# Attention and two gated MLPs in one kernel: the order of the first pairs and its loads, a conversion of float64 weights, and a priority at the end

## The chip, the cores and the metric

The kernel runs on one core of a Trainium2 chip. The metric is the time of one execution on the device in microseconds (us): 707.32 us, the median of three runs before the change (706.92 to 711.9).

## The reference

Three stages follow one another, for 4 batches of 576 positions with width 512.

- Attention with 8 heads of width 64. Heads 0 to 3 see the last 32 positions (local), heads 4 to 7 the earlier positions of the same residue modulo 32 (strided).
- A gated block: `h = gelu(x @ w_in)`, cut into halves u and v; v is normalised and mixed along the positions, `v_s = w_sg @ v_n + b_sg`; the result is `x + (u * v_s) @ w_out`.
- A plain block: `x + relu(norm(x) @ w_ch1) @ w_ch2`, with an inner width of 2048.

The inputs are float32. The weights w_in, w_out, w_ch1 and w_ch2 reach the kernel as float64 words.

## The kernel before, in words

**Matrix products.** Each large operand is split into a high and a low fp32r part (`split`, lines 175 to 181), and a product is three matmuls (`mm3`, lines 203 to 205): low by high, high by low, high by high. Nearly all of TensorE's (PE's) time goes into these.

**Attention** works on pairs of heads, p = 0 and 1 local, p = 2 and 3 strided, per batch. `attn_load` (l) loads queries and keys of a pair into a tile `qk`, 592 KB for a local pair and 601 KB for a strided one; `attn_load_v` (m) loads its values, 432 or 384 KB. `attn_s` (s) makes the scores in two PSUM banks: for batch 0 the mask is written into the bank first, as a matmul of the identity `ident_r` by `mask_lr` or `mask_sr`, with start=True, and the 36 or 44 small products of queries and keys are added. VectorE (DVE) reduces each bank to row maxima (L378), and subtracts them (L380) for p = 0, 2 and 3. `attn_e` (e) takes the exponential on ScalarE (ACT; L394, or L399 one block at a time for p = 1), the row sums (L395), and scales the rows (L402 to L409). `attn2` (x) transposes on PE (L438), copies on ACT (L446), multiplies with the values (L457, L474) and splits the result into `xhl`. Of `qk`, `v` and `pt` there are two buffers each.

**Start of the kernel.** The string START gives the program order of the first steps of batch 0: the letters above with the number of the pair, `w` (load, convert and split one of four 512 KB tiles of w_in for the v half), `v` (12 matmuls of 512 columns for four row blocks with that tile, into four PSUM banks of the pool ps_d), and `c` (constants). START_D names the pairs whose scores use ps_d's four banks instead of ps_s's two. The loads of a step are issued on SyncE's (SP's) queue. With the first pair go four pieces of its queries and keys (the first five blocks of queries, the same of keys, then the rest of both), and ident (64 KB) and mask_l (96 KB) after the first two; mask_s (27 KB) goes in `load_consts`.

**The order on the engines.** A planner puts the instructions of each engine, and the DMA issues of SP, in order when the kernel is built. It goes by the program order as priority and by its own model of when operands and buffers are there; `tc.high_priority(offset=100)` moves the instructions inside it ahead by 100 places in that priority. On the chip each engine runs its list in that order, so an instruction that waits holds up all behind it on its engine. PE's weight loads may run ahead of its matmuls.

**Weights.** `from_f64` (lines 183 to 198) turns a float64 word, read as two 32-bit words, into a float32: ACT takes the absolute value of the high word times 2^-112 (L190), DVE shifts it left by 3 (L193), puts back the sign bit of the high word (L194), and puts in the top three bits of the low word (L196). It is called 8 times for w_in, 8 for w_out (half as wide), 23 times for w_ch1 and w_ch2, and 18 times at half width in `pre_w`, which converts some of these early and stores them in DRAM.

**The rest.** After the start, four loops per batch run: v (five row blocks), u (8 groups), g (8 groups, needs all of wsg) and y (8 groups); the attention of the next batch is put between them at places given by PLACE0 and PLACE. From about 330 us on only the plain block is left: `ch1` and `ch2_mm` in turn for six column chunks of 384 positions; at the end of a chunk `ch2_out` (line 755) multiplies each of four PSUM sums by the reciprocal norm (L757), adds the residual (L759), and stores the last ones (L761).

Of the kernel before, what the change touches and what calls it, by code (L numbers as in the profile page):

```python
# [24 lines left out]
P = 128  # L25
# [49 lines left out]
    6, "x", 3))  # L75
START = "l0 m0 c0 l1 m1 s0 s1 l2 w0 e0 e1 m2 w1 x0 l3 m3 s2 e2 s3 x1 v0 x2 e3 w2 v1 c1 x3 w3 v2 v3"
CUT = 1
START_D = (1, 2)
F64_SCALE = 2.0 ** -112
NCHUNK = NT // CH  # L80
TPC = CH // P
# [65 lines left out]
def mixer_kernel(ctx: ExitStack, tc: tile.TileContext, io, out):  # L147
# [36 lines left out]
    def from_f64(raw, w, src, k, queue=nc.sync, after=None):  # L184
        if src is not None:
            queue.dma_start(out=raw.rearrange("p (k f) -> p k f", k=k), in_=src)
        r3 = raw.rearrange("p (n w) -> p n w", w=2)
        low, high = r3[:, :, 0], r3[:, :, 1]
        wf = w.bitcast(F32)
        first = nc.scalar.activation(wf, high.bitcast(F32), AF.Abs, scale=F64_SCALE)  # L190
        if after is not None:
            tc.add_manual_dep(first.ins, after.ins.name, ORDER, reason="spare time")
        nc.vector.tensor_scalar(out=w, in0=w, scalar1=3, scalar2=None, op0=ALU.logical_shift_left)  # L193
        nc.vector.scalar_tensor_tensor(out=w, in0=high, scalar=0x80000000, in1=w,  # L194
                                       op0=ALU.bitwise_and, op1=ALU.bitwise_or)
        nc.vector.scalar_tensor_tensor(out=w, in0=low, scalar=29, in1=w,  # L196
                                       op0=ALU.logical_shift_right, op1=ALU.bitwise_or)
        return wf.rearrange("p (k f) -> p k f", k=k)
# [35 lines left out]
    def load_consts():  # L234
        nc.sync.dma_start(out=mask_s, in_=io["mask_s"])
        nc.vector.tensor_copy(mask_sr, mask_s)
        nc.vector.memset(neghalf, -0.5)
        nc.vector.memset(eps, 1e-6)
        nc.vector.memset(one.bitcast(F32), 1.0)
        for t in pts:  # L240
            nc.vector.memset(t.rearrange("p (n w) -> p n w", w=SLOT)[:, :, GW:], 0.0)
        nc.vector.memset(vn[64:128, 1, 4, :].bitcast(F32), 1.0)

    def load_w_v(kk):
        raw, w = slot()
        f = from_f64(raw, w, io["w_in"][kk * P:(kk + 1) * P, 2 * WP:4 * WP].unsqueeze(1), 1)
        split(winh[:, kk, WP:], winl[:, kk, WP:], f[:, 0, :])
# [46 lines left out]
    def attn_load(b, p):  # L294
        local = p < NP // 2
        qk = at.tile([P, max(KO + STRIDE + S, KS + NSG * GW)], F32, tag="qk", name="qk")
        kv[b, p] = qk
        src = io["qk_l" if local else "qk_s"][b, p % (NP // 2)]
        if (b, p) == (0, 0):
            cuts = (0, 5 * QB, KO, KO + STRIDE + 5 * QB, src.shape[1])  # L300
            for i in (0, 2, 1, 3):
                cs = slice(cuts[i], cuts[i + 1])
                nc.sync.dma_start(out=qk[:, cs], in_=src[:, cs])
                if i == 2:
                    nc.sync.dma_start(out=ident, in_=io["ident"])
                    nc.sync.dma_start(out=mask_l, in_=io["mask_l"])
            nc.scalar.activation(ident_r, ident, AF.Copy)
            nc.vector.tensor_copy(mask_lr, mask_l)
        else:
            nc.sync.dma_start(out=qk[:, :src.shape[1]], in_=src)  # L310
        if b:
            attn_load_v(b, p)
# [12 lines left out]
    def attn_s(b, p):  # L325
# [23 lines left out]
        mkr = mask_lr[:, 1, :] if local else mask_sr  # L349
        if on_pe:  # L350
            for sl, m, ps3, lo in todo:
                if lo:
                    nc.tensor.matmul(ps3[:, 0, :], lhsT=ident_r, rhs=mask_lr[:, 0, :], start=True, stop=False,
                                     skip_group_check=True)
                nc.tensor.matmul(ps3[:, lo:, :], lhsT=ident_r,
                                 rhs=mkr.unsqueeze(1).to_broadcast([P, m - lo, w]), start=not lo, stop=False,
                                 skip_group_check=True)
        for i in range(n):
            for h in range(2):
# [4 lines left out]
                nc.tensor.matmul(todo[i % 2][2][r0:r0 + 64, i // 2, :], lhsT=qk[hs_, q0:q0 + QB],  # L364
                                 rhs=qk[hs_, k0:k0 + w], start=not on_pe, stop=True,
                                 skip_group_check=True)
        chunks = []
        for sl, m, ps3, lo in todo:
# [386 lines left out]
    def ch2_out(c, d, f1, op_):  # L755
        r = op_.tile([P, CH], F32, tag="o", name="o")
        nc.vector.tensor_tensor(out=r, in0=accs[c, d][:, :CH], in1=rbs[c], op=ALU.mult)  # L757
        y = ys[c][:, d, :]
# [4 lines left out]
    def v_part(kk):  # L763
        for t in range(4):
            v_mm(0, t, kk)

    first = {"l": lambda p: attn_load(0, p), "m": lambda p: attn_load_v(0, p), "s": lambda p: attn_s(0, p), "e": lambda p: attn_e(0, p),
             "x": lambda p: attn2(0, p), "w": load_w_v, "v": v_part,
             "c": lambda i: load_consts() if i == 0 else nc.sync.dma_start(out=g_v, in_=io["g_v"])}
# [112 lines left out]
```

## Time and profile before

| | |
|---|---|
| median of the runs | 707.32 us |
| the profiled execution, its own time | 709.89 us |
| its span on the chip | 708.1 us |
| PE busy | 691.0 us, 98% |
| PE weight loads busy | 664.5 us, 94% |
| DVE busy | 418.7 us, 59% |
| ACT busy | 284.9 us, 40% |
| granted PE clock, mean | 0.994 |
| DMA | 61.30 MB, mean 87 GB/s |

Busy time is counted from an instruction's start to its end; PE's matmuls overlap, so a busy PE may still wait in short stretches. The share of an engine is a mean over stages that differ: DVE and ACT are busy in most of the first 350 us and little later. The span leaves out some time around the execution, 1.8 us here. The slices of the page show PE at half of the first slice of 17.7 us and at nine tenths or more from the second to the last but one.

### The profile page before, as it was taken

What the parts mean: (1) busy time and instruction counts of PE and PEld (TensorE: products, weight loads), DVE (VectorE), ACT (ScalarE), POOL (GpSimd) and SP (SyncE); (2) the same over time, 40 slices, a digit from 0 to 9 for tenths busy, and PEclk for the clock granted to TensorE, in tenths of its full rate; (3) what the DMA queues carried; (4) which work ended last, traced back from release to release, by engine and by line L of the source; (5) the groups of instructions that cost most, each with busy time, mean ns of one, the idle gap of its engine ahead of it and who ended that gap; (6) DMA issues with size and microseconds to landing.
All of it is one profiled execution on the core that took longest, in us unless ns stands there. A gap on an engine that the chain in (4) does not pass through costs nothing.

```text
span 708.1 us, 12770 instructions
## 1 busy us (share of the span) xinstructions
PE 691.0 (98%) x5206; PEld 664.5 (94%) x5206; DVE 418.7 (59%) x892; ACT 284.9 (40%) x746; POOL 25.6 (4%) x26
## 2 busy tenths in 40 slices
PE   5999999999999999999999999999999999999997
PEld 3779979989898999999999999999999999999997
DVE  4889788696877895999873257262336134413113
ACT  2877976392568463465441132131122113211110
POOL 0002011000200020001000000000000000000000
PEclk9899999999999999999999999999999999999999
DMA  8764223457343425244420020200110010001001
GB/s 252 256 192 145 81 81 125 143 164 222 120 130 106 140 88 200 76 155 134 149 90 1 0 89 23 68 1 0 48 43 1 1 45 1 1 1 45 0 1 45
DMA packets 30346, 61.30 MB, mean 87 GB/s; under 512 B 3088, under 2 KB 14352, under 8 KB 30288
## 3 DMA queue, kind: packets, MB, share of 16 engines
q1 hardware_dynamic: 30288, 60.49, 26.8%
q8 instruction: 41, 0.67, 0.4%
q14 instruction: 17, 0.14, 0.1%
HBM read 48.68 MB, written 11.80 MB: 85 GB/s over the span
## 4 chain that ended last, share of the span: by engine, by line
PE 83%; issue 4%; ACT 4%; DVE 4%; DMA 2%; POOL 1%; SPq 1%; POOLq 0%; ACTq 0%
PE ps_o L205 9%; PE ps_o L203 9%; PE ps_o L204 9%; PE ps_h L205 9%; PE ps_h L203 9%; PE ps_h L204 9%; PE ps_v L203 2%; PE ps_y L203 2%; PE ps_v L205 2%; PE ps_y L204 2%; PE ps_y L205 2%; PE ps_v L204 2%; ACT pt L399 2%; PE ps_t L438 2%; PE ps_u L203 2%
## 5 line engine op out<-in xcount | busy, mean ns | idle before, releaser
L744 DVE SCALAR_TENSOR_TENSOR h<-ps_h,h 128x384 fp32r<-128x384 f32 x96 | 52.8, 549 | 182.4 <-ACT h L743 182.2
L743 ACT ACTIVATE h<-ps_h 128x384 fp32r<-128x384 f32 x96 | 46.8, 488 | 229.9 <-PE ps_h L205 229.7
L203 PE MATMUL ps_o<-h,w 128*128 128x384 f32 x384 | 128.4, 334 | 0.0
L203 PE MATMUL ps_h<-xn,w 128*128 128x384 f32 x384 | 128.4, 334 | 0.0
L204 PE MATMUL ps_h<-xn,w 128*128 128x384 f32 x384 | 128.3, 334 | 0.0
L205 PE MATMUL ps_o<-h,w 128*128 128x384 f32 x384 | 128.3, 334 | 0.0
L205 PE MATMUL ps_h<-xn,w 128*128 128x384 f32 x384 | 128.3, 334 | 0.0
L204 PE MATMUL ps_o<-h,w 128*128 128x384 f32 x384 | 128.3, 334 | 0.0
L203 PEld LDWEIGHTS ps_o<-h,w 128*128 128x128 f32 x384 | 72.1, 188 | 0.2 <-DVE o L757 0.2
L203 PEld LDWEIGHTS ps_h<-xn,w 128*128 128x128 f32 x384 | 72.1, 188 | 0.0
L205 PEld LDWEIGHTS ps_h<-xn,w 128*128 128x128 f32 x384 | 72.1, 188 | 0.0
L204 PEld LDWEIGHTS ps_h<-xn,w 128*128 128x128 f32 x384 | 72.1, 188 | 0.0
L204 PEld LDWEIGHTS ps_o<-h,w 128*128 128x128 f32 x384 | 72.1, 188 | 0.0
L205 PEld LDWEIGHTS ps_o<-h,w 128*128 128x128 f32 x384 | 72.1, 188 | 0.0
L203 PE MATMUL ps_g<-wsg,vn 128*128 128x288 f32 x128 | 39.2, 307 | 0.3 <-ACT wsg L177 0.3
L205 PE MATMUL ps_g<-wsg,vn 128*128 128x288 f32 x128 | 38.3, 300 | 0.0
L203 PE MATMUL ps_u<-xhl,winl 128*128 128x288 f32 x128 | 38.1, 298 | 0.1
L203 PE MATMUL ps_y<-gt,wout 128*128 128x288 f32 x128 | 37.8, 298 | 0.0
L204 PE MATMUL ps_g<-wsg,vn 128*128 128x288 f32 x128 | 37.8, 296 | 0.0
L204 PE MATMUL ps_y<-gt,wout 128*128 128x288 f32 x128 | 37.7, 295 | 0.0
L205 PE MATMUL ps_u<-xhl,winh 128*128 128x288 f32 x128 | 37.7, 295 | 0.0
L205 PE MATMUL ps_y<-gt,wout 128*128 128x288 f32 x128 | 37.7, 295 | 0.0
(170 smaller groups left out, 1281.0 us busy)
## 6 DMA issues: line engine op xcount, KB each, us to landing
raw<-in_w_ch SPq DMA_DIRECT2D x23, 512.0 KB, 3.7
qk<-in_qk_s SPq DMA_DIRECT2D x8, 601.0 KB, 4.8
raw_p<-in_w_ch SPq DMA_DIRECT2D x18, 256.0 KB, 3.2
y_scratch<-y SPq DMA_DIRECT2D x16, 288.0 KB, 3.3
yT<-y_scratch SPq DMA_DIRECT2D x6, 768.0 KB, 4.7
out<-yT SPq DMA_DIRECT2D x24, 192.0 KB, 1.9
qk<-in_qk_l SPq DMA_DIRECT2D x7, 592.0 KB, 5.1
st<-in_w_in SPq DMA_DIRECT2D x8, 512.0 KB, 5.2
```

Of the source, the lines that this page charges most:

```text
L203: nc.tensor.matmul(ps, lhsT=ll, rhs=rh, start=first, stop=False)
L204: nc.tensor.matmul(ps, lhsT=lh, rhs=rl, start=False, stop=False)
L205: last_mm[0] = nc.tensor.matmul(ps, lhsT=lh, rhs=rh, start=False, stop=last)
L399: exps.append(nc.scalar.activation(p3[:, i, :], src, AF.Exp, scale=SCALE, bias=mx[:, i:i + 1], accum_out=sm[:, i:i + 1]))
L438: nc.tensor.transpose(ps[:rows, (t - t0) * c:(t - t0 + 1) * c], src, ident)
L743: nc.scalar.activation(h[:, 0, :], o, AF.Relu)
L744: nc.vector.scalar_tensor_tensor(out=h[:, 1, :], in0=o, scalar=0.0, in1=h[:, 0, :], op0=ALU.max, op1=ALU.subtract)
```

## The change

1. START has a new order, and a new step `r`, which issues the load of a w_in tile by itself; `w` then only converts. Pairs 0, 1 and 2 are loaded one after the other ahead of the first values and weights.
2. `qk` has three buffers. ident, mask_l and mask_s are loaded on ACT's queue, and mask_s no longer in `load_consts`.
3. For pair 0 of batch 0 the products of queries and keys come first (the first of each bank with start=True) and the masks are added after them. Pair 2's scores use ps_s instead of ps_d.
4. In `from_f64` the activation is a parametric ReLU instead of the absolute value, with the slope -2^32 for negative words: for these the factor 2^32 is an exponent bit that the shift by 3 takes to the sign's place. The DVE instruction for the sign goes.
5. In `ch2_out` the first multiply has high priority.

```diff
-START = "l0 m0 c0 l1 m1 s0 s1 l2 w0 e0 e1 m2 w1 x0 l3 m3 s2 e2 s3 x1 v0 x2 e3 w2 v1 c1 x3 w3 v2 v3"
+START = "l0 c0 l1 l2 m0 r0 s0 m1 r1 e0 s1 x0 e1 w0 l3 r2 m2 v0 s2 e2 x1 w1 v1 s3 c1 e3 x2 w2 m3 r3 v2 x3 w3 v3"
-START_D = (1, 2)
+START_D = (1,)
+F64_SIGN = -2.0 ** 32
...
-        first = nc.scalar.activation(wf, high.bitcast(F32), AF.Abs, scale=F64_SCALE)
+        first = nc.scalar.activation(wf, high.bitcast(F32), AF.Prelu, scale=F64_SCALE, alpha=F64_SIGN)
...
-        nc.vector.scalar_tensor_tensor(out=w, in0=high, scalar=0x80000000, in1=w,
-                                       op0=ALU.bitwise_and, op1=ALU.bitwise_or)
...
     def load_consts():
-        nc.sync.dma_start(out=mask_s, in_=io["mask_s"])
...
+    def load_raw_v(kk):
+        raw_v[kk] = slot()
+        nc.sync.dma_start(out=raw_v[kk][0].rearrange("p (k f) -> p k f", k=1),
+                          in_=io["w_in"][kk * P:(kk + 1) * P, 2 * WP:4 * WP].unsqueeze(1))
...
-        qk = at.tile([P, max(KO + STRIDE + S, KS + NSG * GW)], F32, tag="qk", name="qk")
+        qk = at.tile([P, max(KO + STRIDE + S, KS + NSG * GW)], F32, tag="qk", name="qk", bufs=3)
...
         if (b, p) == (0, 0):
+            for t, n in ((ident, "ident"), (mask_l, "mask_l"), (mask_s, "mask_s")):
+                nc.scalar.dma_start(out=t, in_=io[n])
...
-                if i == 2:
-                    nc.sync.dma_start(out=ident, in_=io["ident"])
-                    nc.sync.dma_start(out=mask_l, in_=io["mask_l"])
...
-        if on_pe:
+        late = (b, p) == (0, 0)
+
+        def masks():
...
+        if on_pe and not late:
+            masks()
...
-                                 rhs=qk[hs_, k0:k0 + w], start=not on_pe, stop=True,
+                                 rhs=qk[hs_, k0:k0 + w], start=i < 2 if late else not on_pe, stop=not late,
                                  skip_group_check=True)
+        if late:
+            masks()
...
-        nc.vector.tensor_tensor(out=r, in0=accs[c, d][:, :CH], in1=rbs[c], op=ALU.mult)
+        with tc.high_priority(offset=100):
+            nc.vector.tensor_tensor(out=r, in0=accs[c, d][:, :CH], in1=rbs[c], op=ALU.mult)
```

## Rows read from the trace of the kernel before

**Rows 1.** Windows: length, busy us and instructions per engine, PEclk, DMA, GB/s.

```profile
0.00:10.00 10.00, 4.14 (x42) 3.00 (x42) 1.77 (x9) 1.59 (x2) 0.20 (x4) 1.00 0.78 198
10.00:20.00 10.00, 6.09 (x93) 4.75 (x93) 7.83 (x23) 5.94 (x24) 0.00 (x0) 0.99 1.00 331
20.00:30.00 10.00, 9.67 (x135) 8.14 (x136) 8.19 (x25) 8.17 (x21) 0.00 (x0) 0.66 0.59 175
30.00:50.00 20.00, 19.95 (x206) 14.84 (x205) 17.74 (x46) 15.50 (x42) 1.16 (x1) 1.00 0.85 267
50.00:100.00 50.00, 49.28 (x536) 44.23 (x535) 43.07 (x107) 44.04 (x144) 5.61 (x5) 1.00 0.34 107
100.00:400.00 300.00, 297.86 (x2446) 285.89 (x2445) 227.03 (x523) 152.14 (x417) 18.60 (x17) 1.00 0.38 121
400.00:700.00 300.00, 300.00 (x1732) 300.00 (x1731) 108.88 (x157) 57.47 (x100) 0.00 (x0) 1.00 0.06 22
```

**Rows 2.** Timeline of the head: start, us, instruction, idle before and releaser.

```profile
0.73 0.86 SPq L303 DMA_DIRECT2D qk<-in_qk_l  x2
...
4.20 0.31 ACT L307 ACTIVATE ident_r<-ident 128x128 fp32r<-128x128 f32 x1 [2.19 <-DMA ident<-in_ident]
4.48 0.43 SPq L310 DMA_DIRECT2D qk<-in_qk_l  x1
...
5.33 0.42 PE L353 MATMUL ps_sc<-mask_lr,ident_r 128*128 128x96 f32 x1 [5.33 <-DVE mask_lr L308]
...
6.46 1.86 PE L364 MATMUL ps_sc<-qk 64*64 64x96 f32 x36
...
9.47 0.19 DVE L236 CAST mask_sr<-mask_s 128x54 fp32r<-128x54 f32 x1 [4.28 <-DMA mask_s<-in_mask_s]
9.57 1.12 DVE L378 TENSOR_REDUCE mx<-ps_sc 128x4 f32<-128x384 f32 x2
...
12.26 1.87 PE L364 MATMUL ps_sc<-qk 64*64 64x96 f32 x36 [2.79 <-DMA qk<-in_qk_l]
13.89 1.12 DVE L378 TENSOR_REDUCE mx<-ps_sc 128x4 f32<-128x384 f32 x2 [2.17 <-PE ps_sc L364]
...
15.00 0.65 DVE L395 TENSOR_REDUCE sm<-pt 128x5 f32<-128x480 f32 x1
...
17.22 1.33 PE L438 MATMUL ps_t<-ident,pt 128*96 128x128 f32 x8 [0.47 <-DVE pt L409]
...
25.78 0.78 PE L203 MATMUL ps_v<-winh,xhl 128*128 128x512 f32 x1
```

**Rows 3.** Windows: the stretch with a lower clock.

```profile
20.10:27.00 6.90, 6.67 (x95) 5.54 (x97) 5.84 (x15) 5.10 (x12) 0.00 (x0) 0.52 0.65 207
```

**Rows 4.** Timeline: products with the values, pair 0 and pair 1.

```profile
20.33 2.19 PE L457 MATMUL ps_pv<-pT,vt 96*64 96x64 f32 x36 [0.75 <-ACT pT L446]
...
26.86 1.27 PE L457 MATMUL ps_pv<-pT,vt 96*64 96x64 f32 x36
```

**Rows 5.** Groups by line: count, busy us, mean ns, idle before.

```profile
L194 DVE SCALAR_TENSOR_TENSOR w<-raw,w 128x512 uint32<-128x512 uint32 x23 | 15.7, 684 | 0.2
...
L287 ACT ACT_TABLE_LOAD x5 | 6.4, 1283 | 0.1
...
L194 DVE SCALAR_TENSOR_TENSOR st<-st 128x512 uint32<-128x512 uint32 x8 | 5.4, 680 | 0.0
```

**Rows 6.** Windows from the start: GB/s gives the bytes moved.

```profile
0.00:8.50 8.50, 3.17 (x40) 2.54 (x41) 1.24 (x7) 1.59 (x2) 0.20 (x4) 1.00 0.74 176
...
0.00:12.50 12.50, 4.38 (x50) 3.24 (x53) 3.49 (x12) 2.72 (x4) 0.20 (x4) 1.00 0.83 199
0.00:14.50 14.50, 6.38 (x80) 5.01 (x81) 4.10 (x14) 2.72 (x4) 0.20 (x4) 1.00 0.86 216
```

**Rows 7.** Chain of waits: start, us, what.

```profile
45.84 4.29 DMA st<-in_wsg_t
...
78.36 0.49 ACT pT L446
```

More of the change, by code (lines that the diff above doesn't have):

```diff
@@ L242, in load_consts @@
         nc.vector.memset(vn[64:128, 1, 4, :].bitcast(F32), 1.0)
+    raw_v = {}
+    def load_raw_v(kk):
+        raw_v[kk] = slot()
+        nc.sync.dma_start(out=raw_v[kk][0].rearrange("p (k f) -> p k f", k=1),
+                          in_=io["w_in"][kk * P:(kk + 1) * P, 2 * WP:4 * WP].unsqueeze(1))
     def load_w_v(kk):
-        raw, w = slot()
-        f = from_f64(raw, w, io["w_in"][kk * P:(kk + 1) * P, 2 * WP:4 * WP].unsqueeze(1), 1)
+        raw, w = raw_v.pop(kk)
+        f = from_f64(raw, w, None, 1)
         split(winh[:, kk, WP:], winl[:, kk, WP:], f[:, 0, :])
@@ L349, in attn_s @@
         mkr = mask_lr[:, 1, :] if local else mask_sr
-        if on_pe:
+        late = (b, p) == (0, 0)
+        def masks():
             for sl, m, ps3, lo in todo:
                 if lo:
-                    nc.tensor.matmul(ps3[:, 0, :], lhsT=ident_r, rhs=mask_lr[:, 0, :], start=True, stop=False,
+                    nc.tensor.matmul(ps3[:, 0, :], lhsT=ident_r, rhs=mask_lr[:, 0, :], start=not late, stop=late,
                                      skip_group_check=True)
                 nc.tensor.matmul(ps3[:, lo:, :], lhsT=ident_r,
-                                 rhs=mkr.unsqueeze(1).to_broadcast([P, m - lo, w]), start=not lo, stop=False,
-                                 skip_group_check=True)
+                                 rhs=mkr.unsqueeze(1).to_broadcast([P, m - lo, w]), start=not lo and not late,
+                                 stop=late, skip_group_check=True)
+        if on_pe and not late:
+            masks()
         for i in range(n):
@@ L767, in mixer_kernel @@
     first = {"l": lambda p: attn_load(0, p), "m": lambda p: attn_load_v(0, p), "s": lambda p: attn_s(0, p), "e": lambda p: attn_e(0, p),
-             "x": lambda p: attn2(0, p), "w": load_w_v, "v": v_part,
+             "x": lambda p: attn2(0, p), "w": load_w_v, "v": v_part, "r": load_raw_v,
              "c": lambda i: load_consts() if i == 0 else nc.sync.dma_start(out=g_v, in_=io["g_v"])}
```

## The prediction

> **What bounds the kernel now.** I read the windows of the whole span first. From 400 to 700 us TensorE (PE) is busy 300.00 of 300 us and from 100 to 400 us it is idle for 2.14 us, from 50 to 100 us for 0.72 us [rows 1]. The reader is to see that nothing in the last 650 us can be worth more than some 3 us, unless matmuls go away, and the change removes none. The idle time lies in the head: in the first 10 us PE is busy 4.14 us, in the next ten 6.09, in the next 9.67 [rows 1]. That is 5.86 + 3.91 + 0.33 = 10.1 us of idle time, and the column PEclk adds a second loss, 0.66 from 20 to 30 us. So the head decides, and its timeline was read next [rows 2].
>
> It shows four waits. PE's first instruction is a mask matmul at 5.33 us, because the masks are written into PSUM first and mask_lr comes late. DVE's first reduction of pair 0 starts at 9.57 us, although those scores stand in PSUM since about 8.3: ahead of it in DVE's order is the cast of mask_s, which waited 4.28 us for its DMA and ran at 9.47. The keys and queries of pair 1 were issued at 4.48 us behind two sets of values, and PE waits for them until 12.26. And pair 0's row sums run at 15.00, behind the reductions of pair 1, which had to wait for those scores, so that PE's first transposes of pair 0 start only at 17.22 and the first v matmul at 25.78 [rows 2].
>
> **The clock.** From 20.1 to 27.0 us the granted clock is 0.52 of full, the lower level, 1.2 GHz against 2.4 GHz after it, behind a stretch in which PE was busy for 6.09 of 10 us [rows 1, 3]. What it costs is read from the same 36 matmuls at either level: 2.19 us for those of pair 0 at 20.33, 1.27 us for those of pair 1 at 26.86, which ran as the clock came back [rows 4], a ratio of 1.72 or more. At that ratio throughout, the 6.67 us of busy time would lose 6.67 x (1 - 1/1.72) = 2.8 us. The nearest row the other way is the wait for data that hides it: 0. I take 1.5, about half, since part of this stretch waits for ScalarE (ACT) and DVE.
>
> **The change part by part**, against the profiled execution, 709.9 us with a span of 708.1, 2.6 above the median of 707.3 of the runs. The sum is a difference and is taken off the median.
>
> (1) The start of pair 0. Three constants leave SP's queue for ACT's, and the scores come before their masks. One issue on SP takes 0.43 us [rows 2], so the last two of the four pieces go out 0.9 us earlier. PE can begin when the first two pieces are there. They are issued at 0.73 and 1.16; my estimate for the second is about 3.7 us, since ident, issued before behind the two pieces of 0.73, at 1.6, let ACT go on at 4.20 [rows 2], 2.6 us later. PE would start at about 3.9 instead of 5.33: 1.4 us. Bounds: 0 (the masks end the wait after all: ACT now issues three DMAs, 3 x 0.43 = 1.3 us, in front of its table load of 1.28 us [rows 5]) and 2.0 (the second piece lands after no more than ident's wait of 2.19 us [rows 2], at 3.35).
>
> By the Trainium skill, "DMA: Bandwidth & Descriptors", section "Issuing engines are not separate DMA queues", issuing from a second engine saves only the issue time, as the transfers share the same 16 DMA engines; by that rule the move to ACT's queue is worth the 0.9 us of the issues, and with that alone the sum would be 0.5 lower. Before the change no load is on ACT's queue, so no row shows it.
>
> (2) Loads in order of need with a third buffer. Pair 1's queries and keys now stand directly behind pair 0's. What must have moved by then is 592 KB + 187 KB of constants + 592 KB, 1.40 MB. Before, 176 GB/s x 8.5 us = 1.50 MB had moved by 8.5 us, so they land at about 8.5 instead of 12.2; the values of pair 0 behind the third pair's 601 KB (2.46 MB in all) at about 12.5, for 199 x 12.5 = 2.49 MB, and the first weights (2.99 MB) at about 14.3, for 216 x 14.5 = 3.13 MB [rows 6]. Pair 0's scores end at about 7.1 (3.9 + 1.9 for the 36 products of the row at 12.26 + 1.1 for masks, from 5.33 to 6.46). DVE then starts at 6.6 instead of 9.57, and with mask_s out of its way and no reduction of pair 1 in between it needs to the first transposes the old 9.57 to 17.22 less the pause of 2.2 us before 13.89 and the 1.1 us of the reductions behind it: 4.4 us, so 11 us instead of 17.2. The values of pair 0 are late next (12.5), then its weights (14.3 + conversions and splits of some 3 us), so the first v matmul comes at about 18 instead of 25.78.
>
> PE has by then little to do: scores of three pairs, two sets of transposes and products, so not all of these 7.8 us is kept. I count it by idle time. Before, from the start of PE to 30 us, it is 0.53 + 3.91 + 0.33 = 4.8 us [rows 1]. After, I expect 0.4 to 1 us before pair 1's products, up to 1 before the transposes and 1 to 2 around 14 to 18 us, 2.9 in all: 1.9 us gained. Bounds: 0 and 4.8. Behind 30 us PE was busy 19.95 of 20 us before [rows 1], and gains nothing more.
>
> The third buffer lets batch 1's pair go out earlier, in front of weights: 592 KB at 331 GB/s [rows 1] is 1.8 us for each weight tile behind it. I cost it at nothing, because PE has v matmuls of the pairs before it to run; without that cover it is 1.8 us.
>
> (3) The sign. One DVE instruction leaves each conversion: 15.7 us (x23) and 5.4 (x8) [rows 5], and for the 26 conversions of half the width an estimated 26 x 0.34 = 9 us, some 30 us of DVE in all. ACT's instruction keeps its shape and its operands, so I cost it at nothing; the rival D is what speaks against that. In 20 to 100 us, where DVE is busy 69 of 80 us [rows 1], it gives DVE room to follow a PE that is ahead; by itself it is worth at most the 0.72 + 2.14 us that PE is idle after 50 us. I take 0.3, a tenth of it, because these waits are short ones spread over 350 us and DVE is one engine of three that can end them; bounds 0 and 2.9.
>
> (4) Freeing the last sums first. PE is idle 0.00 us from 400 to 700 [rows 1], and the last multiply of the kernel has nothing before it to overtake: so a gain of 0 is all that the row allows. Against it: a multiply put in front of what feeds PE costs one DVE instruction there, on average 108.88 / 157 = 0.69 us [rows 1]. PE's two column blocks of lead cover it; without them it is 0.69 us for each chunk that ends.
>
> Sum: 1.4 + 1.5 + 1.9 + 0.3 = 5.1; I take off 0.3 for the multiply's bound and the buffers of PSUM that pair 2 now shares with pair 0. 4.8 us: **702.5 us** (705.1 against the profiled execution).
>
> **Rivals.** A, the forecast: 702.5, between 700.3 and 704.6 as the clock's term goes from 0 to 2.8 and the idle time from 1 to 4 us.
>
> B, the head closes up altogether: 2.0 + 4.8 + 2.8 = 9.6 us at most; with two thirds of the idle time 2.0 + 3.2 + 2.8 = 8.0, 699.3. For it: DVE and ACT are idle 10.4 and 12.5 of the first 20 us [rows 1]. Against it: the DMA engines, busy 0.78 and 1.00 there, move the same bytes in any order.
>
> C, what PE gains is given back: from 45.8 to past 78 us the chain of waits runs through the load of wsg (4.29 us), then DVE and ACT, and leaves ACT for PE at 78.36 + 0.49 [rows 7]; ACT is busy 44.04 of 50 us from 50 to 100 [rows 1]. If that chain doesn't start earlier, because its load is put later in SP's queue, all is lost but 1 us: 706.3. Against it: the link in front of that load is the Gelu of the v sums, which come earlier, and DVE has 5.4 us less to do for the weights of w_in alone [rows 5].
>
> D, slower: the parametric ReLU isn't in the table that is loaded. Each conversion would then bring a load and one more before the next exponential or Gelu, 2 x 1.28 = 2.57 us. Up to 100 us there are 16 conversions (8 + 8), 41 us; ACT is idle there for 100 - 75.2 = 24.8 us [rows 1], so it decides from the tenth conversion on and costs 16 us at least: 723. Against it: the absolute value and the copies before ran between exponentials and Gelus without a load of their own: the 5 loads shown stand at Gelu's line [rows 5]. The Trainium skill, "ScalarE: Activation LUTs", section "Table sets: the hidden batching unit", names relu, copy, identity and abs as functions in every set, and not this one, and puts a switch at about 2.7 us with its drain; at that price 16 conversions would cost an estimated 85 us before the idle time is taken off.
>
> **How the numbers follow.** A 0.62, B 0.18, C 0.15, D 0.05. The predicted time is A's. The range takes in A, most of B and C: 699.0 to 706.8; it leaves out D, B's last part and the end of C. A measurement of this kernel can tell about 1%, 7.07 us, from no change: faster by that means below 700.25. That is B and the low end of A, 0.2; slower is D, 0.05; the rest, 0.75, is within.
>
> **What would show it.** PE's first instruction near 3.9 us, and a score product, not a mask; pair 1's products near 8.5; first transposes near 11; first v matmul near 18; no stretch at half clock, or a later one. ACT_TABLE_LOAD as often as before. PE busy from 400 to 700 us as before. I am wrong if PE's idle time in the first 30 us stays near 10 us (step 2 or 1 failed), if the gain is there at 45 us and gone at 100 (C), or if any stretch after 100 us changes by more than 2 us.

## The result, and the profile after

The changed kernel takes **713.12 us** (median of 12 runs, 710.65 to 715.12) against 708.03 us before (12 runs, 706.48 to 711.9): a ratio of 1.0065, 95% interval 1.0049 to 1.0081. It is slower by 4.6 us by the ratio and by 5.1 by the medians, within 1%; the forecast was 702.5, 4.8 us faster. The profiled execution of after took 712.14 us, with a span of 709.9 against 708.1.

Windows of after, the same stretches as in [rows 1]:

```profile
0.00:10.00 10.00, 4.70 (x58) 3.81 (x62) 3.13 (x12) 1.59 (x2) 0.20 (x4) 1.00 0.83 244
10.00:20.00 10.00, 8.28 (x129) 6.59 (x121) 8.30 (x26) 7.05 (x28) 0.00 (x0) 0.83 0.93 267
20.00:30.00 10.00, 8.85 (x126) 6.92 (x125) 8.13 (x24) 9.72 (x28) 0.00 (x0) 1.00 0.93 299
30.00:50.00 20.00, 16.75 (x215) 13.13 (x214) 15.86 (x42) 13.56 (x32) 0.10 (x1) 1.00 0.88 249
50.00:100.00 50.00, 48.96 (x511) 44.30 (x510) 39.07 (x94) 43.71 (x143) 4.79 (x5) 1.00 0.35 107
100.00:400.00 300.00, 295.25 (x2421) 283.14 (x2420) 205.62 (x477) 150.22 (x416) 15.89 (x17) 1.00 0.38 118
400.00:700.00 300.00, 300.00 (x1733) 300.00 (x1732) 108.40 (x156) 57.72 (x100) 0.00 (x0) 1.00 0.07 22
```

Read the first busy column, PE. In the first 30 us PE is idle for 5.30 + 1.72 + 1.15 = 8.17 us, 1.9 less than the 10.1 before. Then it loses more than that: 3.25 us of idle time from 30 to 50 us (0.05 before), 1.04 from 50 to 100 (0.72) and 4.75 from 100 to 400 (2.14). The sum is 4.2 us more idle time than before. The spans differ by 1.8 us only. The clock can be one reason, though how much it makes was not measured: the execution of before also ran at the lower clock for 6.9 us [rows 3], and this one for 3.4:

```profile
15.50:18.90 3.40, 3.40 (x43) 2.85 (x41) 2.36 (x8) 3.24 (x12) 0.00 (x0) 0.50 0.96 359
```

Timeline of the head of after (PE and VectorE), against [rows 2]:

```profile
4.11 1.22 PE L373 MATMUL ps_sc<-qk 64*64 64x96 f32 x20 [4.11 <-DMA qk<-in_qk_l]
...
6.52 0.92 PE L373 MATMUL ps_sc<-qk 64*64 64x96 f32 x16 [1.19 <-DMA qk<-in_qk_l]
7.37 0.45 PE L359 MATMUL ps_sc<-mask_lr,ident_r 128*128 128x96 f32 x1
...
8.30 1.12 DVE L389 TENSOR_REDUCE mx<-ps_sc 128x5 f32<-128x480 f32 x2 [1.89 <-PE ps_sc L361]
...
9.37 1.87 PE L373 MATMUL ps_sc<-qk 64*64 64x96 f32 x36
...
11.47 1.10 DVE L406 TENSOR_REDUCE sm<-pt 128x5 f32<-128x480 f32 x2
...
14.05 0.42 PE L449 MATMUL ps_t<-ident,pt 128*96 128x128 f32 x2 [1.14 <-DVE pt L420]
...
21.44 0.93 PE L202 MATMUL ps_v<-winh,xhl 128*128 128x512 f32 x3 [0.46 <-ACT pts L405]
```

PE's first product starts 1.2 us earlier than the first mask matmul did, but it stops for the second pieces of pair 0 until 6.52, and the masks that used to fill this wait come behind it. So the first reduction starts at 8.30, not 6.6. The transposes start at 14.05 instead of 17.22 and the v matmuls at 21.44 instead of 25.78; 11 and 18 were forecast.

Two new waits show in the list of what PE waited for, over the whole of after (total, times, longest):

```profile
PE ps_o L202 <- DVE o L769: 2.4, 1, 2.4
PE ps_v L202 <- ACT g L292: 2.1, 1, 2.1
```

The second is near 46 us (timeline, ScalarE and PE):

```profile
45.40 0.68 ACT L178 ACTIVATE wsg<-st 128x576 fp32r<-128x576 f32 x1 [3.62 <-DMA st<-in_wsg_t]
46.10 1.28 ACT L292 ACT_TABLE_LOAD   x1
47.39 0.60 ACT L292 ACTIVATE g<-ps_v 128x512 f32<-128x512 f32 x1
...
48.04 0.50 PE L202 MATMUL ps_v<-winh,xhl 128*128 128x512 f32 x1 [2.13 <-ACT g L292]
```

The Gelu that frees PE's PSUM bank stands, in ScalarE's list, behind the split of the first wsg tile, and that waits 3.62 us for its DMA. In the kernel before, the split stood behind two Gelus (timeline of before, ScalarE):

```profile
45.59 0.60 ACT L287 ACTIVATE g<-ps_v 128x512 f32<-128x512 f32 x1 [0.97 <-PE ps_v L205]
...
47.16 0.59 ACT L287 ACTIVATE g<-ps_v 128x512 f32<-128x512 f32 x1
50.15 0.69 ACT L177 ACTIVATE wsg<-st 128x576 fp32r<-128x576 f32 x1 [2.41 <-DMA st<-in_wsg_t]
```

The first is near 343 us, in the last stage (timeline, ScalarE, VectorE and PE):

```profile
339.12 1.02 DVE L769 TENSOR_TENSOR o<-ps_o,rb 128x384 f32<-128x384 f32 x2
...
341.57 0.91 ACT L181 ACTIVATE w<-w,g 128x256 fp32r<-128x256 f32 x2 [1.70 <-DMA w<-w_scratch]
342.11 0.89 DVE L182 SCALAR_TENSOR_TENSOR w<-w,g,w 128x256 fp32r<-128x256 f32 x2 [0.91 <-ACT w L181]
342.91 1.02 DVE L771 TENSOR_TENSOR yT<-o,yT 128x384 f32<-128x384 f32 x2
...
344.18 0.55 DVE L769 TENSOR_TENSOR o<-ps_o,rb 128x384 f32<-128x384 f32 x1
...
344.79 0.45 PE L202 MATMUL ps_o<-h,w 128*128 128x384 f32 x1 [2.39 <-DVE o L769]
```

Of the four multiplies that free the sums of the first chunk (L769) two run at 339.12, and the third only at 344.18: between them VectorE's list now has work on weights, and that waits for ScalarE, which waits for a tile to come back from scratch. In the chain of waits of after both places appear, where [rows 7] had the load of wsg alone:

```profile
39.20 6.18 DMA st<-in_wsg_t
...
338.06 3.49 DMA w<-w_scratch
342.11 0.89 DVE w L182 x2
```

### The profile page after: what moved, and what is told of

Read it like the earlier page. It is cut to its first block, busy times and chain, and to the rows that moved or that the text cites. A ratio compares the mean times of both kernels' runs of the same rounds, so it can differ in the third digit from the quotient of the medians.

```text
span 709.9 us, 12712 instructions
## 1 busy us (share of the span) xinstructions
PE 688.6 (97%) x5206; PEld 663.4 (93%) x5206; DVE 393.3 (55%) x835; ACT 283.7 (40%) x746; POOL 21.0 (3%) x26
## 4 chain that ended last, share of the span: by engine, by line
PE 80%; DVE 7%; issue 5%; DMA 4%; ACT 3%; POOL 0%; SPq 0%; POOLq 0%; ACTq 0%
PE ps_o L202 8%; PE ps_o L203 8%; PE ps_o L204 8%; PE ps_h L204 8%; PE ps_h L203 8%; PE ps_h L202 8%; PE ps_y L202 2%; PE ps_y L203 2%; PE ps_y L204 2%; PE ps_v L202 2%; PE ps_v L204 2%; PE ps_v L203 2%; PE ps_u L202 2%; PE ps_u L204 2%; PE ps_u L203 2%
```

## The experiments

Each kernel was timed beside the kernel before, 12 times (e4_noprio 6, g1_after 7); the medians of before beside them were 707.8 to 708.2 us. A ratio is not always the quotient of the two medians: for h1_best to h4_stream_sign that quotient is 0.0012 to 0.0017 higher. Idle is PE's in the profiled execution, us in that window. This is one execution of each kernel and not the median one: that of e3_prio was the fastest of its runs, those of e4_noprio, g2_head_sign and g3_tail_sign the slowest. "Last stage" is the time from the start of the first ps_h matmul to the start of the last ps_o matmul there. "Sign" means the parametric ReLU with the VectorE instruction gone.

| kernel | median us | ratio, 95% interval | idle 35-50 | idle 330-360 | last stage |
|---|---|---|---|---|---|
| before | 708.0 | 1 | 0.05 | 0.00 | 404.4 |
| after | 713.12 | 1.0065 [1.0049, 1.0081] | 2.94 | 2.39 | 406.1 |
| e1_sign | 709.67 | 1.0021 [1.0004, 1.0038] | 0.19 | 1.52 | 405.4 |
| e2_head | 708.72 | 1.0006 [0.9990, 1.0022] | 1.10 | 0.00 | 403.4 |
| e3_prio | 708.99 | 1.0003 [0.9988, 1.0019] | 0.00 | 0.00 | 403.5 |
| e4_noprio | 713.5 | 1.0066 [1.0040, 1.0092] | 2.36 | 2.81 | 408.3 |
| f1_wsg | 709.84 | 1.0035 [1.0017, 1.0052] | 0.80 | 1.86 | 405.9 |
| f2_sums | 709.86 | 1.0022 [1.0002, 1.0042] | 0.81 | 2.07 | 406.0 |
| f3_both | 710.77 | 1.0039 [1.0024, 1.0054] | 0.81 | 2.40 | 406.3 |
| f5_sign_sums | 708.24 | 1.0005 [0.9991, 1.0020] | 0.20 | 1.05 | 405.6 |
| g1_after | 711.95 | 1.0065 [1.0042, 1.0088] | 1.92 | 2.14 | 405.8 |
| g2_head_sign | 707.4 | 0.9991 [0.9973, 1.0010] | 3.14 | 0.00 | 403.8 |
| g3_tail_sign | 711.21 | 1.0043 [1.0027, 1.0058] | 1.16 | 1.57 | 405.6 |
| g4_start | 709.67 | 1.0024 [1.0007, 1.0042] | 0.00 | 0.00 | 403.6 |
| h1_best | 707.5 | 0.9978 [0.9957, 0.9998] | 0.81 | 0.00 | 403.8 |
| h2_sign_twice | 707.83 | 0.9978 [0.9957, 0.9999] | 0.98 | 0.00 | 403.4 |
| h3_pre_sign | 708.29 | 0.9990 [0.9969, 1.0012] | 0.81 | 0.00 | 404.1 |
| h4_stream_sign | 709.75 | 1.0005 [0.9986, 1.0024] | 1.30 | 1.44 | 405.4 |
| i1_old_head | 706.34 | 0.9978 [0.9961, 0.9995] | 0.19 | 0.17 | 404.3 |
| i2_masks_first | 711.75 | 1.0046 [1.0030, 1.0062] | 1.64 | 0.06 | 403.6 |

### The parts alone

**e1_sign**: the kernel before with the sign alone.

```diff
-        first = nc.scalar.activation(wf, high.bitcast(F32), AF.Abs, scale=F64_SCALE)
+        first = nc.scalar.activation(wf, high.bitcast(F32), AF.Prelu, scale=F64_SCALE, alpha=F64_SIGN)
...
-        nc.vector.scalar_tensor_tensor(out=w, in0=high, scalar=0x80000000, in1=w,
-                                       op0=ALU.bitwise_and, op1=ALU.bitwise_or)
```

> The kernel before with the sign alone changed (parametric ReLU, one DVE instruction less for each conversion). Theory 1, the planned order: with shorter conversions the planner spreads the four multiplies at the end of the first chunk among weight conversions on DVE, so PE waits there for the third of them; the head stays as before. Expected 1 to 2.5 us slower than before, with one PE wait of 1.5 to 2.5 us on the multiply near 343 us and no PE wait on Gelu near 46 us. Rival 1, the loads of the head cost the time: within 1 us of before. Rival 2, the parametric ReLU itself costs time: 4 to 5 us slower, with more table loads or longer activations than 0.68 us.

**e2_head**: after with the old sign and without the priority, so the new head alone.

```diff
-        first = nc.scalar.activation(wf, high.bitcast(F32), AF.Prelu, scale=F64_SCALE, alpha=F64_SIGN)
+        first = nc.scalar.activation(wf, high.bitcast(F32), AF.Abs, scale=F64_SCALE)
...
+        nc.vector.scalar_tensor_tensor(out=w, in0=high, scalar=0x80000000, in1=w,
+                                       op0=ALU.bitwise_and, op1=ALU.bitwise_or)
...
-        with tc.high_priority(offset=100):
```

> The changed kernel with the old sign instruction and the old priority, so the head alone (order, third buffer, loads on ACT's queue, late masks). Theory 1: the split of wsg stands behind the first two Gelus on ACT again, so what the head gains is kept: 2 to 4.5 us faster than before, no PE wait on Gelu near 46 us, no wait on the multiply near 343 us. Rival 1, the new order of the loads makes the loads of wsg and the batch-1 tiles late and so gives back the gain whatever stands on ACT: 1 to 4 us slower than before. Rival 2: 1 to 4 us faster.

**e3_prio**: before with the priority alone.

```diff
+        with tc.high_priority(offset=100):
             nc.vector.tensor_tensor(out=r, in0=accs[c, d][:, :CH], in1=rbs[c], op=ALU.mult)
```

> The kernel before with the high priority of the multiply alone. Theory 1 and rival 1: within 1 us of before, PE idle from 300 to 360 us as before (about 0.5 us), since the four multiplies were already close together. Rival 3, the priority moves the multiply in front of what feeds PE: 1 to 3 us slower, with a PE wait at each chunk's end.

**e4_noprio**: after without the priority.

```diff
-        with tc.high_priority(offset=100):
```

> The changed kernel without the high priority of the multiply. Theory 1: as the changed kernel, 711.5 to 714, with the wait near 46 us on Gelu (2 us) and the wait on the multiply near 343 us (1.5 to 2.5 us) both there. Rival 3, the priority is to blame for the wait at the chunk's end: 2 us below the changed kernel, and that wait gone.

The priority is worth nothing either way (1.0003 added, 1.0066 against 1.0065 taken out), and e4's 2.81 us of idle time near 343 us show that it did not bring that wait. The head alone is level (1.0006), where its theory had 2 to 4.5 us gained; the sign alone loses 0.21%, as its theory had. Their sum is 0.27%, and together they lose 0.65%: they interact. The wait near 343 us comes with the sign (e1 has 1.52 us of it, e2 and e3 none). The one near 46 us comes with the two together.

### Mending the two waits by an order

**f1_wsg**: after, with the first splits of wsg ordered behind the second Gelu.

```diff
-                split(wsg[:, 0, s, :], wsg[:, 1, s, :], f)
+                split(wsg[:, 0, s, :], wsg[:, 1, s, :], f, after=gelus[1])
```

> The changed kernel with one thing moved: on ACT the first split of wsg stands behind the second Gelu instead of ahead of the first (an ordering edge; no work is left out). Theory 1: the PE wait on Gelu near 46 us (2.1 us in the changed kernel) goes, and 1.5 to 3 us of the 5.1 come back, so 710 to 711.7 us. Rival 1, the transfers are late anyway and the wait moves to the load of wsg or to the first g group: the wait is gone but less than 0.7 us come back, 712.4 to 713.5.

**f2_sums**: after, with the low halves of w1 tile 6 on VectorE ordered behind the four multiplies of the first chunk.

```diff
+        if c == 0 and f1 < NF - 1 and d == KD - 1:
+            for h in held:
+                tc.add_manual_dep(h.ins, m.ins.name, ORDER, reason="behind the sums")
```

> The changed kernel with the low halves of the seventh w_ch1 tile ordered on DVE behind the four multiplies that free the sums of the first chunk. Theory 1: PE's wait on the multiply near 343 us (2.4 us) goes and 1.5 to 2.5 us come back, 710.6 to 711.6 us. Rival 1: the wait is covered by something else that is late, such as the next weights, and less than 0.7 us come back.

**f3_both**: the two edits together.

```diff
+                split(wsg[:, 0, s, :], wsg[:, 1, s, :], f, after=gelus[1])
...
+                tc.add_manual_dep(h.ins, m.ins.name, ORDER, reason="behind the sums")
```

> The changed kernel with both orderings. Theory 1: both sums add up, 3 to 5 us come back, 708 to 710 us, that is the time of before, with PE idle from 300 to 360 us under 0.7 us and no PE wait on Gelu. Rival 1, the loads: 711 us or more.

**f5_sign_sums**: e1_sign with the second edit.

```diff
+                tc.add_manual_dep(h.ins, m.ins.name, ORDER, reason="behind the sums")
```

> The kernel before with the sign change and with the low halves of the seventh w_ch1 tile ordered behind the four multiplies. Theory 1: the 1.5 us that the sign change alone cost were the wait at the chunk's end, so this is at before or up to 1.5 us below it, 706.5 to 708.3 us. Rival 4, a shorter conversion is worth nothing or costs elsewhere in the middle of the kernel: 709 us or more with the wait gone.

Each edit is faster than after by 0.3 to 0.4%, both together by no more (their theory had 708 to 710 us), and none reaches the kernel before. f5_sign_sums is 0.16% under e1_sign, with overlapping intervals, and still has 1.05 us of the wait. The edit at the sums did what it says, all four multiplies ran between 336.41 and 340.4 us, but PE still waited there: 2.07 us of idle time from 330 to 360, 1.25 of them for one of these multiplies. They now stand behind an earlier tile from scratch, and VectorE has work without a break from there to the last of them, as the timeline of f2_sums shows (ScalarE, then VectorE):

```profile
333.17 0.91 ACT L183 ACTIVATE w<-w,g 128x256 fp32r<-128x256 f32 x2 [3.30 <-DMA w<-w_scratch]
...
333.71 0.89 DVE L184 SCALAR_TENSOR_TENSOR w<-w,g,w 128x256 fp32r<-128x256 f32 x2 [3.26 <-ACT w L183]
```

The wait for that tile is no new one; after has it too (ScalarE):

```profile
335.88 0.91 ACT L181 ACTIVATE w<-w,g 128x256 fp32r<-128x256 f32 x2 [3.22 <-DMA w<-w_scratch]
```

So mending one place in a list was no test of the cause, and the next runs changed what makes the list.

### Which conversions, and the instruction or the order

**g1_after**: after, unaltered, as a control beside the next kernels.

> The changed kernel again, unaltered, beside this call's other kernels. Theory (two waits, near 46 us and near 343 us, are in its written-out order, so every execution has them): 713 us (711.5 to 714.5), 1.005 to 1.009 of the kernel before; PE idle 2.4 to 3 us in 35 to 50 us and 2.2 to 2.9 us in 330 to 345 us. Rival (the first call's chip condition made it look slower than the kernels of the second call): 709.5 to 711, under 1.004.

**g2_head_sign**: after with the sign in w_in and w_out alone (HEAD_PRELU is True, and these conversions are called with head=True).

```diff
+        if head is HEAD_PRELU:
             first = nc.scalar.activation(wf, high.bitcast(F32), AF.Prelu, scale=F64_SCALE, alpha=F64_SIGN)
+        else:
+            first = nc.scalar.activation(wf, high.bitcast(F32), AF.Abs, scale=F64_SCALE)
...
+        if head is not HEAD_PRELU:
+            nc.vector.scalar_tensor_tensor(out=w, in0=high, scalar=0x80000000, in1=w,
+                                           op0=ALU.bitwise_and, op1=ALU.bitwise_or)
```

> All of the change, but the parametric ReLU only in the conversions of w_in and w_out; the streamed weights (w_ch1, w_ch2) keep the magnitude and the separate sign operation. Theory: the wait near 343 us belongs to the streamed conversions, the wait near 46 us to the head's, so PE idle in 330 to 345 us falls to under 0.3 us (after: 2.39) and 35 to 50 us keeps 2 to 3 us idle, since the planned order has the split of wsg ahead of the first Gelu as in the changed kernel; 710.5 to 712, 1.002 to 1.005 of before. Rival (the two are one thing, such as the shorter conversions being late everywhere): 330 to 345 us keeps over 1 us idle and the ratio stays over 1.005.

**g3_tail_sign**: the converse, in w_ch1 and w_ch2 alone.

```diff
-HEAD_PRELU = True
+HEAD_PRELU = False
```

> The converse: all of the change, but the parametric ReLU only for the streamed weights; w_in and w_out keep the separate sign operation. Theory: the planned order then has the split of wsg behind the first Gelus, so PE idle in 35 to 50 us is 0.5 to 1.2 us (after: 2.94), and 330 to 345 us keeps 1 to 2.9 us idle, the four multiplies of the first chunk being planned apart; 709.5 to 711.5, 1.002 to 1.004 of before. Rival (the wait near 46 us comes from the new head's loads and not from the place of the split): 35 to 50 us keeps over 2 us idle.

The control stays at 1.0065. Without the sign in the streamed weights the whole loss is gone (0.9991), and with it there alone most of it stays (1.0043). The idle time near 343 us went as the theory had it. But g2_head_sign's median is level with before, so the theory's 710.5 to 712 was wrong. Its profile has the wait near 46 us in full, 3.14 us of idle time from 35 to 50 us; that execution was the slowest of its twelve, 710.31 us, and PE ran at the lower clock behind the wait:

```profile
48.40:51.90 3.50, 3.13 (x8) 2.51 (x8) 3.50 (x12) 2.29 (x5) 1.00 (x1) 0.51 0.88 276
```

So this profile does not tell what the wait costs the median execution.

**h1_best**: g2_head_sign with f1_wsg's order.

```diff
-                split(wsg[:, 0, s, :], wsg[:, 1, s, :], f)
+                split(wsg[:, 0, s, :], wsg[:, 1, s, :], f, after=gelus[1])
```

> The new head with the parametric ReLU only in w_in and w_out (g2_head_sign), and the first split of wsg held behind the second Gelu, as in f1_wsg. Theory (the wait of ScalarE for wsg near 46 us is 2 us of the end): PE idle in 35 to 50 us falls from 3.1 to under 1.2 us, 330 to 345 us stays at 0; 705 to 706.5, 0.995 to 0.998 of before. Rival (what the wait costs there is made up before the batch's end, since 50 to 100 us has idle time of its own): 707 to 708, within 0.1% of g2_head_sign.

**h2_sign_twice**: after, with the old VectorE instruction put back for the streamed weights, beside the parametric ReLU.

```diff
         first = nc.scalar.activation(wf, high.bitcast(F32), AF.Prelu, scale=F64_SCALE, alpha=F64_SIGN)
...
+        if head is not HEAD_PRELU:
+            nc.vector.scalar_tensor_tensor(out=w, in0=high, scalar=0x80000000, in1=w,
+                                           op0=ALU.bitwise_and, op1=ALU.bitwise_or)
```

> The changed kernel with the parametric ReLU everywhere, and for the streamed weights also the removed sign operation on VectorE, which then sets a bit that is set already. Theory (the loss is the order written for the shorter conversion): the planned order is that of g2_head_sign, so 330 to 345 us has under 0.3 us idle and the time is 706.5 to 708.5, 0.998 to 1.001 of before. Rival (the ReLU itself costs in the last stage): 711 to 713, over 1.004, with over 1 us idle in 330 to 345 us.

**h3_pre_sign**: g2_head_sign with the sign also in the nine prepared tiles.

```diff
-                f = from_f64(raw, w, None, 1, after=last_mm[0])
+                f = from_f64(raw, w, None, 1, after=last_mm[0], head=True)
```

> The parametric ReLU in w_in, w_out and in the nine streamed tiles that are prepared during the batches (100 to 295 us); the tiles converted in the last stage keep the sign operation. Theory (the loss is where the last stage's own conversions got shorter): the four multiplies stand together in the planned order, 330 to 345 us has under 0.3 us idle, 706.5 to 709. Rival (the shorter preparation moves the stores to scratch or the reloads from it): over 1 us idle in 300 to 360 us and 710 or more.

**h4_stream_sign**: g2_head_sign with the sign also in the 23 tiles converted for the last stage.

```diff
-            f = from_f64(raw, w, w_src(i, j), 2).rearrange("p k f -> p (k f)")
+            f = from_f64(raw, w, w_src(i, j), 2, head=True).rearrange("p k f -> p (k f)")
```

> The converse of h3_pre_sign: the parametric ReLU in w_in, w_out and in the streamed tiles that are converted in the last stage; the nine prepared ones keep the sign operation. Theory: the four multiplies are planned apart (places 614, 614, 620, 624 on VectorE), 330 to 345 us has 1 to 2.9 us idle, 710 to 712.5, 1.003 to 1.006 of before. Rival (the preparation is what costs): 708.5 or less and 330 to 345 us under 0.5 us idle.

h2_sign_twice is the run that decides. It executes the parametric ReLU everywhere and one VectorE instruction more per streamed tile than after, and it is faster than after, 0.9978 against 1.0065. In the traces it has the instructions of g2_head_sign in the same order on all five engines, from first to last, with the other function in the streamed conversions, and these two are level (0.9978 and 0.9991, with overlapping intervals). **The instruction costs nothing; the order written for the shorter conversion does.** h3_pre_sign narrows it: in the traces its order is that of after on SP from first to last, on ScalarE and VectorE until the first streamed tiles are converted for the last stage (at 232 us in after), and on PE until 325 us. The edit between the two is the one instruction in 23 conversions, and the times are 0.9990 and 1.0065. On PE the lists differ around 325 us, by the place of two small matmuls (ps_r), and at the end of the first chunk: after leaves the sums after 6 of 12 matmuls, turns to ps_h for 5 and comes back, while h3_pre_sign, as before, takes them by twelve. The same stretch as above, in the timeline of h3_pre_sign (ScalarE and VectorE):

```profile
336.71 0.55 DVE L776 TENSOR_TENSOR o<-ps_o,rb 128x384 f32<-128x384 f32 x1
...
337.96 0.55 DVE L776 TENSOR_TENSOR o<-ps_o,rb 128x384 f32<-128x384 f32 x1
...
339.83 1.01 DVE L776 TENSOR_TENSOR o<-ps_o,rb 128x384 f32<-128x384 f32 x2
...
341.07 0.91 ACT L182 ACTIVATE w<-w,g 128x256 fp32r<-128x256 f32 x2 [0.62 <-DMA w<-w_scratch]
341.61 0.89 DVE L183 SCALAR_TENSOR_TENSOR w<-w,g,w 128x256 fp32r<-128x256 f32 x2 [0.30 <-ACT w L182]
```

All four multiplies are done by 340.84, before the work that waits for scratch begins, and PE's windows show no idle time (h3_pre_sign first, then after):

```profile
330.00:360.00 30.00, 30.00 (x175) 30.00 (x174) 26.57 (x52) 15.48 (x32) 0.00 (x0) 1.00 0.50 158
```

```profile
330.00:360.00 30.00, 27.61 (x159) 27.12 (x158) 22.39 (x45) 15.62 (x32) 0.00 (x0) 1.00 0.44 141
```

The reader is to see that VectorE, in the third busy column, is busier in the faster kernel, 26.57 against 22.39 us.

h4_stream_sign, which differs from after in the nine prepared tiles alone, has the wait (1.44 us) and loses 0.14% to g2_head_sign, less than its theory had (1.003 to 1.006 of before) and not clear of the intervals. So the two uses do not add up: 0.9990 and 1.0005 each, 1.0065 together. h1_best has no wait for wsg ahead of the Gelus and 0.81 us of idle time from 35 to 50 us; its 707.5 us are its rival's (707 to 708), not its theory's (705 to 706.5).

### What the head is worth

**g4_start**: before with the constants on ScalarE's queue and the masks of pair 0 behind its products.

```diff
+            for t, n in ((ident, "ident"), (mask_l, "mask_l"), (mask_s, "mask_s")):
+                nc.scalar.dma_start(out=t, in_=io[n])
...
+        late = (b, p) == (0, 0)
...
+        if late:
+            masks()
```

> The kernel before with one part of the head alone: the constants ident, mask_l and mask_s loaded on ScalarE's queue and pair 0's masks behind its products; the order of the first steps, two query/key buffers and the sign as before. Theory (the start is worth about half a microsecond, since the masks only change places with the products and the second pieces land at 6.5 us): first product at 4.1 to 4.3 us, first reduction 8.2 to 8.6 us (8.97 in the before-like heads with the other edits alone, 9.57 before), PE idle in the first 20 us 7.7 to 8.3 us (8.4 to 8.8 there), no new wait later; 0.998 to 1.000 of before, 706.5 to 708.2. Rival (the earlier start is what disturbs the later order): an idle stretch of over 1 us between 35 and 100 us, ratio 1.001 or more. Rival (the forecast's full 1.4 us are there): 706.5 or less.

**i1_old_head**: before with the sign in w_in and w_out alone.

```diff
+        if head:
+            first = nc.scalar.activation(wf, high.bitcast(F32), AF.Prelu, scale=F64_SCALE, alpha=F64_SIGN)
+        else:
             first = nc.scalar.activation(wf, high.bitcast(F32), AF.Abs, scale=F64_SCALE)
...
+        if not head:
+            nc.vector.scalar_tensor_tensor(out=w, in0=high, scalar=0x80000000, in1=w,
+                                           op0=ALU.bitwise_and, op1=ALU.bitwise_or)
```

> The kernel before (old order of the first steps, two query/key buffers, masks first) with the parametric ReLU in w_in and w_out alone. Theory (the new head is worth under 1 us, because ScalarE is busy throughout 20 to 35 us and the loads take the same bytes): 707.3 to 708.7, 0.998 to 1.001 of before, at most 1 us over h1_best's 707.5; first Gelu at 40.5 to 44 us and 0 to 0.4 us of PE idle in 35 to 50 us. Rival (the head is worth what the forecast gave it and only the sign's loss hid it): 709 or more, 1.5 us or more over h1_best.

**i2_masks_first**: h1_best with the masks of pair 0 ahead of its products.

```diff
-        late = (b, p) == (0, 0)
+        late = False
```

> h1_best with pair 0's masks ahead of its products, as in the kernel before; the constants still come by ScalarE's queue. Theory (the late masks only swap places with the products and the second pieces of pair 0 land at 6.5 us either way): first reduction 8.3 to 9.0 us, first transposes within 0.5 us of h1_best's (14.7), 706.8 to 708.2, within 0.1% of h1_best. Rival (the late masks are worth the 1.4 us of the forecast's first term): 708.5 or more, with the first reduction at 9.4 us or later.

i1_old_head is at 0.9978 without a line of the new head, faster than its theory had, and h1_best at 0.9978 with all of it: the head is worth nothing that these runs can tell, as e2_head's 1.0006 said. g4_start had its first product at 4.08 and its first reduction at 8.51, as expected, but 8.66 us of idle time in the first 20 us, where 7.7 to 8.3 were expected, and its ratio was 1.0024 [1.0007, 1.0042], its median 1.7 us above before. Its profiled execution, with a span of 706.4, does not show why.

i2_masks_first was meant to price the late masks and priced something else. Its first reduction came earlier, at 7.38 us, since pair 0's masks now filled PE's time before the products, but the list came out with the conversion of the first w_in tile ahead of pair 1's exponentials, and ScalarE stood (timeline, ScalarE):

```profile
9.00 1.17 ACT L416 ACTIVATE pt<-pt 128x384 f32<-128x384 f32 x2 [5.19 <-DVE pt L402]
15.26 0.66 ACT L195 ACTIVATE st<-st 128x512 f32<-128x512 f32 x1 [5.09 <-DMA st<-in_w_in]
15.82 0.32 ACT L421 ACTIVATE pt<-ps_sc,mx 128x96 f32<-128x96 f32 x1
```

That is 5.09 us for one DMA, a first v matmul at 27.05 us instead of h1_best's 21.96, and a median 4.2 us over h1_best's. It is the pattern of the other two waits once more, though no run mends this wait and so prices it. What the late masks are worth stays open.

## Why the prediction was wrong

Two things failed, each by some 5 us. The head's three terms, 1.4 + 1.5 + 1.9 = 4.8 us, are the whole forecast, and the head alone gave nothing: e2_head is at 1.0006 [0.9990, 1.0022], so at most an estimated 0.001 x 708 = 0.7 us can be there. And the sign, priced at a small gain, was the loss.

**The step that made the kernel slower is (3), the sign**: "I take 0.3, a tenth of it [...]; bounds 0 and 2.9." VectorE's busy time did fall, by 25.4 us (418.7 to 393.3) where some 30 were reckoned, and the part in w_in and w_out is a gain: 0.22% with the old head (i1_old_head), and 0.15% with the new one (g2_head_sign against e2_head), the latter within the intervals. That is 1.1 to 1.6 us where 0.3 were forecast. In the streamed weights it is a loss: 0.75% from h3_pre_sign to after, an estimated 0.0075 x 708 = 5.3 us (3.7 to 4.8 by the medians, 708.29 against 711.95 and 713.12), on the side that the bounds left out. The step counted freed time on an engine whose list is written ahead, and took the list as given. Shorter conversions are planned earlier and closer, and an instruction that waits for a load then stands in front of one that PE needs.

Of this the profiles show 2.0 and 1.7 us in the last stage (406.1 in after and 405.8 in g1_after, against 404.1), where PE's idle time is 2.39 and 2.14 us. The last matmul starts 3.3 and 2.4 us later than in h3_pre_sign, but 1.6 and 1.0 of that stand at 230 us already, where the lists are still the same: that much is the spread of executions. A further part may be the clock, which fell behind that wait in e4_noprio's profiled execution, to the lower level, 1.2 GHz (0.53), for 3.4 us with PE busy throughout:

```profile
345.50:348.90 3.40, 3.40 (x13) 3.40 (x12) 3.40 (x8) 2.23 (x4) 0.00 (x0) 0.53 0.34 86
```

The mean granted clock of after's 12 runs is 0.9944 and that of h3_pre_sign's 0.9968. At most 0.0024 x 708 = 1.7 us would follow from that, but no profiled execution of after itself has such a stretch in the last stage, so this is argued and not shown. The rest stays open, and so does why the prepared and the streamed tiles lose more together than apart.

**(1) the start, 1.4.** The first product came at 4.11 us, 3.9 forecast. What failed is the link from it to VectorE: the second pieces land at 6.5 us and the masks follow them, so the first reduction was 1.3 us earlier than in before's profiled execution and about 0.7 earlier than in other executions of the old head (8.97 in e1_sign, 8.98 in e3_prio).

**(2) the order, 1.9.** Pair 1's products at 9.37 us, 8.5 forecast; the gain of 1.9 us in PE's idle time to 30 us is there to the tenth, against this one execution. Against others it is luck: the five profiled kernels with the old head (before, e1_sign, e3_prio, f5_sign_sums, i1_old_head) have 8.4 to 10.1 us of idle time up to 30 us, 9.2 in the mean, and the thirteen with the new head (all but g4_start and i2_masks_first) 7.4 to 10.1, 8.8 in the mean. In after the gain was given back by 50 us, with 3.2 us more idle time from 30 to 50. ScalarE was the engine that this step left out: it is busy 9.72 of 10 us from 20 to 30, and the first v matmul waits for it last. That it holds the head back is argued from this and not tested. (One sum of the step is off: 3.9 + 1.9 + 1.1 is 6.9, not 7.1.)

**The clock, 1.5.** The stretch at the lower level was no property of the old head: e1_sign and e3_prio, with the same head, have none in the first 50 us, f5_sign_sums has one from 12.5 to 22.7 us, and new heads have it too (after 15.5 to 18.9, e2_head 14.2 to 21.1). Nor was the late first v matmul: 25.78 us in the execution that was read, 22.6 in e1_sign and e3_prio. The three terms of the head were sized on one execution that started worse than its kernel does.

**(4)** was right: 0.

**Rivals.** A's ends do not follow from its terms: 1.4 with a clock of 0 to 2.8 and idle time of 1 to 4 gives 704.9 to 699.1, not 704.6 to 700.3; the range is wider than either. C, the gain given back, named wsg, and wsg's load does hold the chain in after; but its mechanism was SP's queue, and what stood in the way was a place in ScalarE's list. Its price in the medians is small: h1_best takes the wait out and is 0.13% under g2_head_sign, with overlapping intervals. D is refuted. The groups of after show as many table loads as [rows 5], and the parametric ReLU takes as long as the absolute value did (669 against 672 ns; after first, then before):

```profile
L191 ACT ACTIVATE w<-raw 128x512 f32<-128x512 f32 x23 | 15.3, 669 | 9.0 <-DMA raw<-in_w_ch 4.1 <-DVE w L179 2.7 <-DVE w L182 2.0
...
L292 ACT ACT_TABLE_LOAD x5 | 6.4, 1283 | 0.1
```

```profile
L190 ACT ACTIVATE w<-raw 128x512 f32<-128x512 f32 x23 | 15.3, 672 | 16.2 <-DMA raw<-in_w_ch 7.8 <-DVE w L178 3.5 <-DVE w L196 2.2
```

The Trainium skill, "ScalarE: Activation LUTs", section "Table sets: the hidden batching unit", does not name this function among those of every set; in this kernel it behaves as one of them. Of the signs given, two spoke in after's profile. "Any stretch after 100 us changes by more than 2 us": 2.6 us more idle time from 100 to 400. And that of C, a gain at 45 us that is gone at 100: PE's idle time up to 45 us is 9.3 us against 10.2 before, and up to 100 us 12.5 against 10.9.

No kernel of these beats the one before by much. i1_old_head, 706.34 us and 0.9978 [0.9961, 0.9995], has the lowest median: the sign in w_in and w_out and nothing else of the change.

## What to carry to other kernels

Where a planner writes each engine's list ahead of time, an instruction made shorter or taken out is not just time given back: it moves others, and the price is what now stands behind a wait for a DMA. So compare the two lists before pricing the edit, and look for any instruction that frees a PSUM bank for PE and has come to stand behind one that waits for a load. To separate the instruction from the order, keep the old instruction beside the new one: if that kernel is the faster, the order is the cause. And do not size the start of a kernel on one execution, when other kernels or runs with the same start can be read.

## What was not expected of the hardware

The first wsg tile's arrival differs by up to 3.8 us between executions of kernels whose lists are the same up to there: ScalarE's split of it started at 45.40 us in after, 44.03 in g1_after, 46.13 in g2_head_sign, 42.94 in h2_sign_twice, 42.38 in h3_pre_sign and 44.63 in h4_stream_sign. The load was issued between 38.6 and 39.8 us in these six and landed 3.7 to 6.6 us later, so the spread is in the transfer and not in the issue; what makes it was not found. The wait near 46 us is as long as that load is late, 0.91 to 3.81 us on ScalarE, and one profile of it says little of its mean: g2_head_sign and h2_sign_twice have the same lists, and the spans of their profiled executions are 708.5 and 704.0 us.
